# Eight attention batches and their expert layer on one core: the second softmax turned by way of DRAM instead of on TensorE, and batch 0's state read moved into batch 1

## The chip, the cores and the metric

The kernel runs on one core of a Trainium2 chip. The core has a matrix engine (TensorE, PE in the profile, with PEld for its weight loads), a vector engine (VectorE, DVE), a scalar engine (ScalarE, ACT), GpSimd (POOL) and SyncE (SP), which here only issues DMAs. The metric is the device time of one execution in microseconds (us); lower is better. The kernel before takes 654.04 us, the median of 3 runs (653.77 to 654.39).

## The reference, cut to what matters

An attention between 512 tokens and 32 state rows, both ways, for 8 batches of 8 heads of 64 numbers, and then one expert layer over all 4352 rows (512 tokens and 32 state rows of each batch), with 512 inputs, 2048 hidden numbers and 512 outputs:

```python
scores = scale * np.matmul(x, state.transpose(0, 1, 3, 2))     # x: 8, 8, 512, 64
a = softmax(scores)                                            # state: 8, 8, 32, 64
xread = np.matmul(a, state)
scores2 = scale * np.matmul(state, x.transpose(0, 1, 3, 2))
a2 = softmax(scores2)
sread = np.matmul(a2, x)
rows = np.concatenate([xread, sread], axis=2)                  # per head: 512 + 32 rows
...
h = rows @ w_in                                                # 512 -> 2048
g = np.where(h >= 1, h, np.where(h <= -1, 0.0, (h + 1) ** 2 / 4))
return g @ w_out                                               # 2048 -> 512
```

All of it is float32. scores2 is scores turned; both softmaxes work from the same numbers.

## The kernel before, in words

**Precision.** A float32 product is made of three passes with shorter factors: each operand is kept as a high part (h) and a rest (l), and high times high, high times rest and rest times high are summed in PSUM. So every product stands in the rows as three matmuls: L446 to L448 for the first layer (g1, output h), L504 to L506 for the second (g2, output acc).

**Attention folded into the weights.** xread @ w_in is a @ (state @ w_in). So for each batch the kernel forms sw = state @ w_in (`sw_pair`, L393), splits it (swh, swl), and g1 multiplies the first softmax (its high part ath and its rest atl, tokens on the columns) by sw. The first softmax goes on DVE and ACT: `turn` (L237) turns 32x32 blocks of the scores out of PSUM, then maximum, difference, exp, sum, division (top1 to norm1), `back` (L276) turns the result back, `high1` and `rest` split it. The hidden activation follows on ACT and DVE: relu (L455), square (L458), bound (L462), high part gh (L468), rest gl (L473).

**The second softmax**, the one that the change is about, runs over the tokens, which lie on the columns of the scores tile sc: `top2` (L294, L295) takes the maximum of a row on DVE, `exp2` (L298) writes exp and its sum on ACT into the tile e2, state rows on partitions. To read x with it, the tokens must lie on the partitions. `turn2` (L309) does that on TensorE: eight 128x128 transposes per batch into a PSUM tile e2p, which `keep_turned` (L313) copies back over e2 on ACT. Then `read2` (L327) multiplies it with xn, the batch's x with tokens on partitions, in 32 matmuls into sr; `scale2` (L335) divides by the sum; `keep2` (L341) turns the 128x128 result on TensorE; `keep` (L346) stores it in srT. After the last batch the 256 state rows collected in srT pass through the expert layer as a ninth batch of half the steps.

**Steps.** The 2048 hidden numbers are taken in 8 steps j of 256 each. A step has 12 matmuls 128x512 of g1 and 24 of g2; g2 of a step follows g1 of the next, in two parts with other PE work between them (sw of a later step, scores and read2 of a batch).

**Order of the work.** Batches 1 to 8 are written as a loop over steps (b, j), in which the framework's scheduler sets the order on each engine. Batch 0 has a hand-written order: `Plan` holds a list of operations, each with engine, cost, what it waits for and which buffers it takes; the table `ORDER` names them in the order of emission by their number and engine letter; `Plan.times` (from L63) works out a modelled start for each; `Plan.emit` issues them sorted by that start and puts dummy matmuls into warmed (`warm`, L175, "fills") where the model leaves PE idle between the first scores and the first g2. In this stretch the weights come in on SP's queue, 1 MB at a time: raw_i0 to raw_i7 (w_in) in two buffers of the pool rawp, raw_o0 to raw_o7 (w_out) in eight buffers of wop. Each is 64-bit data that two operations turn into float32 halves (`low` L545/L550 on DVE or ACT, `high` L558 on ACT) and that DVE joins (L566) into w32 (w_in) or into wf, a tile of the pool "tmp" (w_out), from which `part_high` (L573, ACT) and `part_low` (L577, DVE) make the two parts of wo, in a buffer of wop again. xt is x for the scores, sb the state, xn x for read2; each comes on SP's queue.

The dictionary `between` says with which step of batch 0 the attention's own PE work is listed: `turn2` of batch 0 with step 0, `read2` with step 1 (between the two halves of g2 of step 0), the scores of batch 1 with step 2, `keep2` with step 3, and `turn2` of batch 1 with step 4.

**PSUM.** Two tiles for h (one of two banks in batch 0), four for acc, and one tile mm of two banks that scores, sw, e2p, sr of batch 0 and rt take in turn.

Of the kernel before, what the change touches and what calls it, by code (L numbers as in the profile page):

```python
# [108 lines left out]
def state_exchange_moe(  # L109
# [91 lines left out]

    class Attention:
# [82 lines left out]

        def top2(self, q):
            b = self.b
            if q == 0:
                tag = "tmp" if b == 0 else "e2"
                self.e2 = work.tile([P, 2, S], F32, tag=tag, bufs=2 if b == 0 else 1, name=f"e2_{b}")  # L290
                self.nm2 = small.tile([P, 2], F32, tag="nm2", name=f"nm2_{b}")
                self.sum2 = small.tile([P, 2], F32, tag="sum2", name=f"sum2_{b}")
# [1 line left out]
            nc.vector.tensor_reduce(out=nm, in_=self.sc[q], op=ALU.max, axis=AX.X, negate=True)  # L294
            nc.vector.tensor_scalar_mul(nm, nm, SCALE)  # L295

        def exp2(self, q):
            nc.scalar.activation(  # L298
                out=self.e2[:, q], in_=self.sc[q], func=AF.Exp, bias=self.nm2[:, q:q + 1],
                scale=SCALE, accum_out=self.sum2[:, q:q + 1],  # L300
            )

        def turn2(self):
            b, e2 = self.b, self.e2
            e2p = self.e2p = ps_mm(f"e2p{b}")
            for q in range(2):
                for t in range(NT):
                    cols = slice(t * P, (t + 1) * P)
                    nc.tensor.transpose(out=e2p[:, q, cols], in_=e2[:, q, cols], identity=ident)  # L309

        def keep_turned(self):
            b = self.b
            nc.scalar.copy(out=self.e2, in_=self.e2p)  # L313
# [558 lines left out]
```

## Time and profile before

| what | value |
|---|---|
| median of 3 runs | 654.04 us (653.77 to 654.39) |
| the profiled execution's own time | 653.93 us |
| its span (first to last instruction) | 651.9 us |
| PE busy | 642.5 us, 99% of the span |
| PEld busy | 521.2 us, 80% |
| ACT busy | 362.3 us, 56% |
| DVE busy | 338.1 us, 52% |
| the chain that ended last | PE 96%, DVE 2%, ACT 1% |
| DMA | 43.64 MB, mean 67 GB/s |

The profile is one execution, taken by the hardware profiler. A row of the trace gives start and length in us, engine, line of the kernel, operation, out<-in by the program's names, and the shape; a release in brackets says how long the engine was idle before the instruction and what ended that. Matmuls overlap, so the lengths of neighbouring matmuls add up to more than the time between their starts. A row of groups gives busy time and mean length in ns, and behind the second bar the idle time just before the group's instructions. A row of stretches gives the window, its length, then for PE, PEld, DVE, ACT and POOL busy us and number of instructions, then the TensorE clock that was granted as a share of full speed, the DMA engines' share and GB/s.

### The profile page before, as it was taken

What the parts mean: (1) busy time and instruction counts of PE and PEld (TensorE: products, weight loads), DVE (VectorE), ACT (ScalarE), POOL (GpSimd) and SP (SyncE); (2) the same over time, 40 slices, a digit from 0 to 9 for tenths busy, and PEclk for the clock granted to TensorE, in tenths of its full rate; (3) what the DMA queues carried; (4) which work ended last, traced back from release to release, by engine and by line L of the source; (5) the groups of instructions that cost most, each with busy time, mean ns of one, the idle gap of its engine ahead of it and who ended that gap; (6) DMA issues with size and microseconds to landing.
All of it is one profiled execution on the core that took longest, in us unless ns stands there. A gap on an engine that the chain in (4) does not pass through costs nothing.

```text
span 651.9 us, 10329 instructions
## 1 busy us (share of the span) xinstructions
PE 642.5 (99%) x4438; PEld 521.2 (80%) x4438; DVE 338.1 (52%) x484; ACT 362.3 (56%) x474; POOL 0.8 (0%) x7
## 2 busy tenths in 40 slices
PE   7999999999999999999999999999999999999997
PEld 6777887878787887878787887878787878788895
DVE  5999958533584338443574339343663334334431
ACT  5999766554565456454664457444664464444632
POOL 0000000000000000000000000000000000000000
PEclk9999999999999999999999999999999999999999
DMA  8996005000400004000500014000300010000101
GB/s 347 387 401 253 1 10 185 0 1 2 168 27 1 1 32 163 0 2 2 193 2 1 1 46 149 1 2 1 130 1 1 0 67 1 0 2 1 64 1 33
DMA packets 11085, 43.64 MB, mean 67 GB/s; under 512 B 1312, under 2 KB 1440, under 8 KB 7968
## 3 DMA queue, kind: packets, MB, share of 16 engines
q1 hardware_dynamic: 6096, 34.28, 13.6%
q10 hardware_dynamic: 4944, 8.72, 3.6%
q8 instruction: 34, 0.56, 0.4%
q14 instruction: 11, 0.09, 0.0%
HBM read 34.08 MB, written 8.91 MB: 66 GB/s over the span
## 4 chain that ended last, share of the span: by engine, by line
PE 96%; DVE 2%; ACT 1%; DMA 0%; issue 0%; POOL 0%; SPq 0%; DVEq 0%; POOLq 0%
PE acc L504 19%; PE acc L505 19%; PE acc L506 19%; PE h L446 10%; PE h L447 10%; PE h L448 10%; PE sw L393 5%; PE sc L230 1%; PE warmed L175 1%; PE sr L327 1%; PE e2p L309 1%; DVE w L566 0%; DVE u L462 0%; DMA out_dram<-o 0%; DVE z L237 0%; DVE z L252 0%
## 5 line engine op out<-in xcount | busy, mean ns | idle before, releaser
L504 PE MATMUL acc<-wo,gh 128*128 128x512 f32 x544 | 214.0, 393 | 0.0
L505 PE MATMUL acc<-wo,gh 128*128 128x512 f32 x544 | 212.1, 390 | 0.0
L506 PE MATMUL acc<-wo,gl 128*128 128x512 f32 x544 | 211.9, 390 | 0.0
L455 ACT ACTIVATE u<-h,half 128x512 f32<-128x512 f32 (+1 forms) x128 | 91.7, 717 | 178.3 <-PE h L448 170.2
L462 DVE SCALAR_TENSOR_TENSOR u<-u,h 128x512 f32<-128x512 f32 (+1 forms) x128 | 86.4, 714 | 199.8 <-ACT u L458 199.6
L504 PEld LDWEIGHTS acc<-wo,gh 128*128 128x128 f32 x544 | 102.2, 188 | 24.4 <-issue 3.3
L506 PEld LDWEIGHTS acc<-wo,gl 128*128 128x128 f32 x544 | 102.1, 188 | 21.6
L505 PEld LDWEIGHTS acc<-wo,gh 128*128 128x128 f32 x544 | 102.2, 188 | 20.6 <-DVE wo L577 0.2
L473 DVE TENSOR_TENSOR gl<-u,gh 128x1024 fp32r<-128x1024 f32 x68 | 83.2, 1224 | 56.5 <-ACT gh L468 56.5
L468 ACT CAST gh<-u 128x1024 fp32r<-128x1024 f32 x68 | 71.5, 1052 | 66.0 <-DVE u L462 63.4
L458 ACT ACTIVATE u<-u 128x1024 f32<-128x1024 f32 x68 | 72.1, 1061 | 1.8
L393 PE MATMUL sw<-w,sb 64*32 64x256 f32 x1024 | 32.3, 380 | 2.5 <-DVE w L566 2.5
L393 PEld LDWEIGHTS sw<-w,sb 64*32 64x32 f32 x1024 | 18.2, 106 | 11.9 <-DVE u L462 2.5
L519 ACT COPY o<-acc 128x512 f32<-128x512 f32 x33 | 19.0, 583 | 12.1 <-PE acc L506 12.1
L446 PE MATMUL h<-ath,sw_3h 128*128 128x512 f32 x64 | 25.1, 393 | 0.0
L446 PE MATMUL h<-ath,sw_5h 128*128 128x512 f32 x64 | 25.0, 391 | 0.0
L447 PE MATMUL h<-ath,sw_5l 128*128 128x512 f32 x64 | 24.9, 389 | 0.0
L448 PE MATMUL h<-atl,sw_5h 128*128 128x512 f32 x64 | 24.9, 389 | 0.0
L447 PE MATMUL h<-ath,sw_3l 128*128 128x512 f32 x64 | 24.9, 389 | 0.0
L448 PE MATMUL h<-atl,sw_3h 128*128 128x512 f32 x64 | 24.9, 389 | 0.0
L446 PE MATMUL h<-ath,sw_1h 128*128 128x512 f32 x60 | 24.4, 407 | 0.5 <-DVE u L462 0.5
L447 PE MATMUL h<-ath,sw_1l 128*128 128x512 f32 x60 | 23.4, 391 | 0.0
(158 smaller groups left out, 722.5 us busy)
## 6 DMA issues: line engine op xcount, KB each, us to landing
xt<-in_xt_dram SPq DMA_DIRECT2D x16, 512.0 KB, 5.2
raw_i<-in_moe_w_in_dram SPq DMA_DIRECT2D x8, 1024.0 KB, 7.0
raw_o<-in_moe_w_out_dram SPq DMA_DIRECT2D x8, 1024.0 KB, 11.4
xn<-in_x_dram SPq DMA_DIRECT2D x8, 1024.0 KB, 6.1
out_dram<-o ACTq DMA_DIRECT2D x32, 256.0 KB, 2.0
sb<-in_state_dram SPq DMA_DIRECT2D x1, 448.0 KB, 8.5
out_dram<-o SPq DMA_DIRECT2D x4, 64.0 KB, 1.7
out_dram<-o ACTq DMA_DIRECT2D x4, 64.0 KB, 2.0
```

The costliest lines, as they stand in the source:

```text
L393: nc.tensor.matmul(banks[hh][pr * NS:(pr + 1) * NS, cols], lhsT=sb[rows, b, pr], rhs=w32[c][rows, pr], start=True, stop=True,)
L446: nc.tensor.matmul(o, lhsT=wh[:, k, sl], rhs=ah[:, k], start=first, stop=False)
L447: nc.tensor.matmul(o, lhsT=wl[:, k, sl], rhs=ah[:, k], start=False, stop=False)
L448: nc.tensor.matmul(o, lhsT=wh[:, k, sl], rhs=al[:, k], start=False, stop=last)
L455: nc.scalar.activation(out=u, in_=h, func=AF.Relu, scale=0.5, bias=half)
L458: nc.scalar.activation(out=self.u, in_=self.u, func=AF.Square)
L462: nc.vector.scalar_tensor_tensor(out=u, in0=u, scalar=1.0, in1=h, op0=ALU.min, op1=ALU.max)
L468: nc.scalar.copy(out=gh, in_=self.u)
L473: nc.vector.tensor_tensor(out=gl, in0=self.u, in1=gh.bitcast(F32), op=ALU.subtract)
L504: nc.tensor.matmul(a, lhsT=lh, rhs=oh, start=f == 0, stop=False)
L505: nc.tensor.matmul(a, lhsT=lh, rhs=ol, start=False, stop=False)
L506: nc.tensor.matmul(a, lhsT=ll, rhs=oh, start=False, stop=f == NF - 1)
```

## The change

Three things change together.

**The block trade, all batches.** `turn2` and `keep_turned` go. In their place `trade` issues DMAs on SP's queue: e2 is stored to a DRAM tile e2d (one store of 128x1024; two of 512 KB in all for batch 0), and four loads bring it back as e2x, a tile of the pool "tmp", so that each quarter of 128 tokens lies on its own 32 partitions with the pairs of heads side by side. `turn_traded` then turns 32x32 blocks of the whole 128x1024 tile in one DVE instruction, which gives tokens on partitions, written over e2. To match, x is laid out on the host with token 128 t + 32 j + k at partition 32 t + k, group j (the DMA of xn has the same size), and exp2 of batches 1 to 7 writes e2 with the two halves of the heads interleaved by quarters. The trade is issued right after exp2, the DVE turn stands where turn2 was called (`first`, step 2 of the batch before). The number of e2 buffers goes from one to two.

**Batch 0.** ACT copies its scores aside (`aside`) from PSUM to e2_0, so that PSUM is free; top2 and exp2 work there in place, later. read2, scale2, keep2 and keep of batch 0 leave the hand-written part and stand behind those of batch 1, in steps 0 and 1 of batch 1. They share the PSUM bank of sr1 and the tile of rt1. `between` keeps only the scores of batch 1. xn0 takes a buffer of rawp and is loaded behind all weights.

**The order.** A new table ORDER; `emit` issues the operations in the table's order, not sorted by their modelled start. The operation "table" (a copy of one column) stands last for ACT. The space for DMA descriptors is given as 8192.

The diff without most of the table, and without what only passes names on:

```diff
@@ ORDER @@
-    "0S 87P 86A 1S 2S 88P 6S 97D 90D 89P 91D 99D 92D 10S 93D 100D 94D 3A 98D 101D 95A 33S 102A 96D "
+    "0S 87P 88P 90D 1S 89P 113A 97D 91D 2S 98D 99D 92D 100D 116A 121A 93D 6S 101D 3A 102A 4D 94D 95A "
...
@@ Plan.emit @@
-        for k in sorted(begun, key=lambda k: begun[k]):
+        for k in begun:
...
@@ load_xn @@
-        xn = work.tile([P, NT, H, D], F32, tag="xn", bufs=1, name=f"xn{b}")
+        if b:
+            xn = work.tile([P, NT, H, D], F32, tag="xn", bufs=1, name=f"xn{b}")
+        else:
+            xn = rawp.tile([P, NT, H, D], F32, tag="raw", name=f"xn{b}")
...
@@ Attention @@
+        def aside(self, q):
+            if q == 0:
+                self.e2 = work.tile([P, 2, S], F32, tag="e2", name=f"e2_{self.b}")
+            nc.scalar.copy(out=self.e2[:, q], in_=self.sc[q])
...
         def exp2(self, q):
+            if self.b:
+                o, i = self.e2[:, :, q], self.sc[q].rearrange("p (t k) -> p t k", k=P)
+            else:
+                o = i = self.e2[:, q]
...
-        def turn2(self):
-            b, e2 = self.b, self.e2
-            e2p = self.e2p = ps_mm(f"e2p{b}")
-            for q in range(2):
-                for t in range(NT):
-                    cols = slice(t * P, (t + 1) * P)
-                    nc.tensor.transpose(out=e2p[:, q, cols], in_=e2[:, q, cols], identity=ident)
-
-        def keep_turned(self):
+        def trade(self):
+            self.e2x = work.tile([P, NPR, 2 * P], F32, tag="tmp", name=f"e2x{self.b}")
+            there = dram.tile([P, NT, 2 * P], F32, tag="e2d", name=f"e2d{self.b}")
+            if self.b:
+                nc.sync.dma_start(out=there, in_=self.e2.rearrange("p t q k -> p t (q k)"))
+            else:
+                for q in range(2):
+                    nc.sync.dma_start(
+                        out=there[:, :, q * P:(q + 1) * P], in_=self.e2[:, q].rearrange("p (t k) -> p t k", k=P)
+                    )
+            for t in range(NT):
+                nc.sync.dma_start(
+                    out=self.e2x[t * NS:(t + 1) * NS], in_=there[:, t].rearrange("(r n) k -> n r k", n=NS)
+                )
+
+        def turn_traded(self):
+            e2 = self.e2.rearrange("p t q k -> p (t q k)" if self.b else "p q s -> p (q s)")
+            nc.vector.transpose(out=e2, in_=self.e2x.rearrange("p r k -> p (r k)"))
+            self.turned = e2.rearrange("p (r q j n) -> p r q j n", q=2, r=NPR, n=NS)
+            self.inv2()
...
             for q in range(2):
                 self.exp2(q)
+            self.trade()
...
-            self.turn2()
-            self.keep_turned()
+            self.turn_traded()
...
@@ att_ops2 @@
+                op(("aside",) + k, "ACT", 0.66, m("aside", q), [("sc", b, 1)] + [("aside", b, 0)] * q, take=take, ends=[("sc", b)])
...
+        op(("trade", b), "SP", 6.5, m("trade"), [("exp2", b, 0), ("exp2", b, 1)], take=[("tmp", ("e2x", b))])
+        op(("kept", b), "DVE", 1.3, m("turn_traded"), [("trade", b)], ends=[("e2x", b)])
...
@@ the loads @@
-    read(("xn", 0), 2.6, load, "xn", load_xn, 0, take=[("xn", ("xn", 0))])
...
+    weights = [k for k in plan.ops if k[0] == "dma" and k[1] in ("i", "o")]
+    read(("xn", 0), 2.6, load, "xn", load_xn, 0, take=[("raw", ("xn", 0))], after=weights)
...
@@ between @@
-        0: lambda: tensor(("e2p", 0), 0.92, lambda: atts[0].turn2(), [("exp2", 0, 0), ("exp2", 0, 1)],
-                          take=[("mm", ("e2p", 0))]),
-        1: lambda: tensor(("sr", 0), 1.23, lambda: atts[0].read2(), [("kept", 0), ("dma", "xn", 0)],
-                          take=[("mm", ("sr", 0))], ends=[("e2", 0), ("xn", 0)]),
...
-        3: lambda: tensor(("rt", 0), 0.15, lambda: atts[0].keep2(), [("rs", 0)], take=[("mm", ("rt", 0))]),
-        4: lambda: tensor(("e2p", 1), 0.92, lambda: atts[1].turn2(), [("exp2", 1, 0), ("exp2", 1, 1)],
-                          take=[("mm", ("e2p", 1))]),
...
@@ the loop over steps (b, j), j = 0 and j = 1 @@
-                atts[b].read2()
-                atts[b].scale2()
+                for k in (1, 0) if b == 1 else (b,):
+                    atts[k].read2()
+                for k in (1, 0) if b == 1 else (b,):
+                    atts[k].scale2()
...
@@ _laid_out @@
-        "x": x.reshape(B, H, S // 128, 128, D).transpose(0, 3, 2, 1, 4),
+        "x": x.reshape(B, H, 4, S // 128, 32, D).transpose(0, 2, 4, 3, 1, 5).reshape(B, 128, S // 128, H, D),
```

Lines of the changed kernel lie some 33 further down: a g2 matmul of L504 to L506 is L537 to L539 there, g1 L479 to L481, scores L235, read2 L358.

What that moves on the engines is seen at three places. First PE in batch 0, from the end of h of step 1 to the first g2 products, before (acc0_0 is the first output tile of g2, wo0 the weights of step 0, gh0_0 and gl0_0 the parts of its activation, e2p0 the turned second softmax):

```order
L448 MATMUL h0_1_297<-atl0_118,sw0_1h_235 128x512
L309 MATMUL e2p0_319<-ident_76,e2_0_247 128x128 x8
L504 MATMUL acc0_0_334<-wo0_314,gh0_0_304 128x512
L505 MATMUL acc0_0_334<-wo0_314,gh0_0_304 128x512
L506 MATMUL acc0_0_334<-wo0_314,gl0_0_305 128x512
L504 MATMUL acc0_1_335<-wo0_314,gh0_0_304 128x512
```

and in the same place after:

```order
L481 MATMUL h0_1_298<-atl0_117,sw0_1h_252 128x512
L537 MATMUL acc0_0_321<-wo0_270,gh0_0_292 128x512
L538 MATMUL acc0_0_321<-wo0_270,gh0_0_292 128x512
L539 MATMUL acc0_0_321<-wo0_270,gl0_0_293 128x512
L537 MATMUL acc0_1_322<-wo0_270,gh0_0_292 128x512
```

The eight turns are gone, and g2 follows h of step 1 at once. Twelve rows further down, before, the read of batch 0 (sr0) stood between the two halves of g2(0, 0) and h of step 2 begins behind it; after, the second half of g2(0, 0) follows the first and then h of step 2.

Second, PE at the first h of batch 1 and at the read of batch 1, before (sc2 are the scores of batch 2, sr1 the read of batch 1):

```order
L505 MATMUL acc0_3_337<-wo6_744,gh0_6_789 128x512
L506 MATMUL acc0_3_337<-wo6_744,gl0_6_790 128x512
L446 MATMUL h1_0_0_888<-ath1_466,sw0_7h_678 128x512
...
L506 MATMUL acc0_3_337<-wo7_821,gl0_7_871 128x512
L327 MATMUL sr1_946<-xn1_579,e2_1_495 32x64 x32
L393 MATMUL sw1_1_0_981<-w32_1_91,sb_88 32x256
```

and after:

```order
L538 MATMUL acc0_3_324<-wo6_684,gh0_6_763 128x512
L539 MATMUL acc0_3_324<-wo6_684,gl0_6_764 128x512
L235 MATMUL sc2_1017<-xt2_846,sb_90 32x512
L479 MATMUL h1_0_0_850<-ath1_420,sw0_7h_639 128x512
...
L539 MATMUL acc0_3_324<-wo7_828,gl0_7_833 128x512
L358 MATMUL sr1_908<-xn1_737,e2_1_473 32x64 x32
L358 MATMUL sr1_908<-xn0_616,e2_0_142 32x64 x32
L426 MATMUL sw1_1_0_977<-w32_1_93,sb_90 32x256
...
L426 MATMUL sw1_3_1_998<-w32_4_96,sb_90 32x256
L235 MATMUL sc2_1017<-xt2_846,sb_90 32x512 x7
L479 MATMUL h1_1_0_1061<-ath1_420,sw1_1h_979 128x512
```

The read of batch 0 stands behind that of batch 1. One of the eight score matmuls of batch 2 has come to stand alone ahead of h of batch 1; the other seven stand where all eight stood.

Third, the end of the weights on SP's queue (what a DMA waits for before it is issued is in brackets, by semaphore), before:

```order
L538 DMA raw_i7_544<-in_moe_w_in_dram 128x2048 [waits DMAHW7_49,DMAHW5_49,DVE_49]
L538 DMA raw_o5_564<-in_moe_w_out_dram 128x2048 [waits DMAHW6_49]
L199 DMA xn1_579<-in_x_dram 128x2048 [waits PE_49]
L194 DMA xt2_884<-in_xt_dram 128x1024 [waits DMAHW0_49,PE_49]
L194 DMA xt2_884<-in_xt_dram 128x1024 [waits DMAHW1_49]
```

and after:

```order
L571 DMA raw_i7_544<-in_moe_w_in_dram 128x2048 [waits DMAHW0_49,DVE_49]
L196 DMA xt2_846<-in_xt_dram 128x1024 [waits DMAHW5_49,PE_49]
L196 DMA xt2_846<-in_xt_dram 128x1024 [waits DMAHW6_49]
L571 DMA raw_o5_613<-in_moe_w_out_dram 128x2048 [waits DMAHW7_49,DVE_49,Activation_49]
L204 DMA xn0_616<-in_x_dram 128x2048 [waits DMAHW2_49]
L323 DMA e2d1_708<-e2_1_473 128x1024 [waits DMAHW1_49]
L330 DMA e2x1_707<-e2d1_708 32x4x256 [waits DMAHW1_49,DVE_49]
L330 DMA e2x1_707<-e2d1_708 32x4x256 [waits DMAHW3_49]
L330 DMA e2x1_707<-e2d1_708 32x4x256 [waits DMAHW4_49]
```

xt2 moves ahead of the last weight, that weight now waits for another engine, and xn0 and the trades of batches 1 and 0 stand behind it.

More of the change, by code (lines that the diff above doesn't have):

```diff
@@ L288, in top2 @@
             if q == 0:
[L289 to L292, printed above, removed]
+                if b:
+                    self.e2 = work.tile([P, NT, 2, P], F32, tag="e2", name=f"e2_{b}")
+                first = "" if b else "_0"
+                self.nm2 = small.tile([P, 2], F32, tag=f"nm2{first}", name=f"nm2_{b}")
@@ L311, in keep_turned @@
-        def keep_turned(self):
+                out=o, in_=i, func=AF.Exp,
+                bias=self.nm2[:, q:q + 1], scale=SCALE, accum_out=self.sum2[:, q:q + 1],
+            )
+        def trade(self):
[12 more added lines that the diff above has]
+                )
@@ L312, in keep_turned, with inv2 @@
+        def turn_traded(self):
[3 more added lines that the diff above has]
+            self.inv2()
+        def inv2(self):
             b = self.b
-            nc.scalar.copy(out=self.e2, in_=self.e2p)
-            self.r2 = small.tile([P, 2], F32, tag="r2", name=f"r2_{b}")
+            self.r2 = small.tile([P, 2], F32, tag="r2" if b else "r2_0", name=f"r2_{b}")
@@ L320, in read2 @@
             xn = loaded.pop(("xn", b))
-            sr = banks[1].tile([P, 512], F32, tag="h", name=f"sr{b}") if b else ps_mm(f"sr{b}")[:, 0]
-            sr = self.sr = sr[:, :2 * D].rearrange("p (q d) -> p q d", q=2)
+            if b:
+                self.read = banks[1].tile([P, 512], F32, tag="h", name=f"sr{b}")
+            else:
+                self.read = atts[1].read
+            at = 0 if b else 2 * D
+            sr = self.sr = self.read[:, at:at + 2 * D].rearrange("p (q d) -> p q d", q=2)
             for q in range(2):
-                for t in range(NT):
+                for j in range(NT):
                     for pr in range(NPR):
-                        c0 = t * P + pr * NS
                         nc.tensor.matmul(
-                            sr[pr * NS:(pr + 1) * NS, q], lhsT=self.e2[:, q, c0:c0 + NS],
-                            rhs=xn[:, t, 2 * pr + q], start=t == 0, stop=t == NT - 1,
+                            sr[pr * NS:(pr + 1) * NS, q], lhsT=self.turned[:, pr, q, j],
+                            rhs=xn[:, j, 2 * pr + q], start=j == 0, stop=j == NT - 1,
                         )
@@ L339, in keep2 @@
         def keep2(self):
-            self.rt = ps_mm(f"rt{self.b}")
+            b = self.b
+            self.turned2 = ps_mm(f"rt{b}") if b else atts[1].turned2
+            self.rt = self.turned2[:, 0 if b else 1, :P]
             nc.tensor.transpose(
-                out=self.rt[:, 0, :P], in_=self.rs.rearrange("p a d -> p (a d)"), identity=ident
+                out=self.rt, in_=self.rs.rearrange("p a d -> p (a d)"), identity=ident
             )
@@ L648, in att_ops2 @@
             k = (b, q)
-            take = [("tmp" if b == 0 else "e2", ("e2", b))] if q == 0 else []
-            op(("top2",) + k, "DVE", 0.8, m("top2", q), [("sc", b) if b else ("sc", b, 1)] + [("top2", b, 0)] * q, take=take)
-            op(("exp2",) + k, "ACT", 0.66, m("exp2", q), [("top2",) + k], ends=[("sc", b)])
-        op(("kept", b), "ACT", 0.95, m("keep_turned"), [("e2p", b)], ends=[("e2p", b)])
-        if b == 0:
-            op(("rs", b), "DVE", 0.25, m("scale2"), [("sr", b)], ends=[("sr", b)])
-            op(("srT", b), "ACT", 0.3, m("keep"), [("rt", b)], ends=[("rt", b)])
+            take = [("e2", ("e2", b))] if q == 0 else []
+            if b:
+                ready, used = [("sc", b)], [("sc", b)]
+            else:
+                op(("aside",) + k, "ACT", 0.66, m("aside", q), [("sc", b, 1)] + [("aside", b, 0)] * q, take=take, ends=[("sc", b)])
+                take, ready, used = [], [("aside", b, q)], []
+            op(("top2",) + k, "DVE", 0.8, m("top2", q), ready + [("top2", b, 0)] * q, take=take)
+            op(("exp2",) + k, "ACT", 0.66, m("exp2", q), [("top2",) + k], ends=used)
+        op(("trade", b), "SP", 6.5, m("trade"), [("exp2", b, 0), ("exp2", b, 1)], take=[("tmp", ("e2x", b))])
+        op(("kept", b), "DVE", 1.3, m("turn_traded"), [("trade", b)], ends=[("e2x", b)])
     hid = {}
@@ L734, in state_exchange_moe @@
     att_ops2(0)
-    op(("sc done", 0), "ACT", 0, lambda: None, [("exp2", 0, 0), ("exp2", 0, 1)])
+    op(("sc done", 0), "ACT", 0, lambda: None, [("aside", 0, 0), ("aside", 0, 1)])
     sw_ops((0, 0))
@@ L812, in state_exchange_moe @@
         elif j == 1:
-            atts[b].keep2()
-            atts[b].keep()
+            for k in (1, 0) if b == 1 else (b,):
+                atts[k].keep2()
+            for k in (1, 0) if b == 1 else (b,):
+                atts[k].keep()
         elif j == 2 and nxt:
```

15 lines of the change are left out of this document (8 added, 7 removed), and 22 rows, old and new, of the table ORDER.

## The prediction

> **What bounds the kernel now.** I read the page first, then the busy time by stretches, then the instructions of TensorE (PE) one by one around each place that the change touches. Starts are us from the span's start.
>
> ```profile
> span 651.9 us, 10329 instructions
> PE 642.5 (99%) x4438; PEld 521.2 (80%) x4438; DVE 338.1 (52%) x484; ACT 362.3 (56%) x474; POOL 0.8 (0%) x7
> PE 96%; DVE 2%; ACT 1%; DMA 0%; issue 0%; POOL 0%; SPq 0%; DVEq 0%; POOLq 0%
> ...
> 40.00:50.00 10.00, 10.00 (x56) 7.37 (x55) 9.88 (x13) 9.96 (x10) 0.00 (x0) 1.00 0.98 387
> 100.00:172.50 72.50, 72.50 (x521) 58.41 (x513) 35.42 (x54) 38.59 (x54) 0.00 (x0) 1.00 0.12 44
> ```
>
> The chain that ended last is 96% PE. The stretches (behind the window: PE, PEld, DVE, ACT, POOL, clock, DMA share, GB/s) show two regimes. From 100 us on a batch takes 72.5 us, PE is busy in all of it, DVE and ACT in half: there a TensorE instruction less is worth its pitch, and work on other engines costs nothing. While the weights come in (40 to 50 us is shown) PE, DVE, ACT and DMA are all full: there PE gains from work taken off it only as far as the others deliver earlier too.
>
> **The turns that go.** A busy PE overstates matmuls, which overlap, so each block is costed by the pitch of its neighbours. First the pitch, then the block of batch 2, then that of batch 0 (start, length):
>
> ```profile
> 37.49 0.39 PE L504 MATMUL acc<-wo,gh 128*128 128x512 f32 x1
> ...
> 39.99 0.39 PE L506 MATMUL acc<-wo,gl 128*128 128x512 f32 x1
> ```
> ```profile
> 117.67 0.39 PE L506 MATMUL acc<-wo,gl 128*128 128x512 f32 x1
> 117.90 1.03 PE L309 MATMUL e2p<-ident,e 128*128 128x128 f32 x8
> 118.69 0.48 PE L504 MATMUL acc<-wo,gh 128*128 128x512 f32 x1
> ...
> 119.24 0.40 PE L506 MATMUL acc<-wo,gl 128*128 128x512 f32 x1
> ```
> ```profile
> 28.08 0.39 PE L448 MATMUL h<-atl,sw_1h 128*128 128x512 f32 x1
> 28.31 1.03 PE L309 MATMUL e2p<-ident,e 128*128 128x128 f32 x8
> 29.10 0.48 PE L504 MATMUL acc<-wo,gh 128*128 128x512 f32 x1
> ...
> 30.05 0.40 PE L504 MATMUL acc<-wo,gh 128*128 128x512 f32 x1
> ```
>
> Twelve matmuls, eleven steps in 2.50: 0.227 us a step. From 117.67 to 119.24 are 1.57 us with three ordinary steps (0.68) in them: a block of eight turns costs 0.89. **Batches 1 to 7: 7 x 0.89 = 6.23 us off.** Batch 0: 28.08 to 30.05 is 1.97, less four steps (0.91), so 1.06.
>
> The Trainium skill (TensorE: Matmul & The Clock Gate, Back-to-back issue gap) gives about 81 ns for a matmul of 128 columns in a stream of loads and matmuls; by it eight blocks of eight would be worth 5.2 us. The trace has 0.79 us from a block's start to the next matmul, 0.10 a turn, before the edges: the row decides.
>
> Batch 0's block also covered a wait, since the g2 behind it needs gl0_0 and wo0:
>
> ```profile
> 20.84 0.70 DVE L545 TENSOR_SCALAR raw_i<-raw_i 128x1024 int32<-128x1024 uint32 x1 [0.65 <-DMA raw_i<-in_moe_w_in_dram]
> 27.06 1.21 DVE L473 TENSOR_TENSOR gl<-u,gh 128x1024 fp32r<-128x1024 f32 x1
> 28.20 1.22 DVE L577 TENSOR_TENSOR wo<-wf,wo 128x1024 fp32r<-128x1024 f32 x1
> ```
> ```profile
> 21.96 1.10 ACT L455 ACTIVATE u<-h,half 128x1024 f32<-128x1024 f32 x1
> ```
> ```profile
> L298 ACT ACTIVATE e<-sc,nm 128x512 f32<-128x512 f32 x16 | 10.9, 684 | 1.7 <-DVE nm L295 1.7
> L313 ACT COPY e<-e2p 128x1024 f32<-128x1024 f32 x8 | 8.1, 1014 | 0.1
> L294 DVE TENSOR_REDUCE nm<-sc 128x1 f32<-128x512 f32 x16 | 10.2, 665 | 0.0
> ```
>
> raw_i2 lands at 20.84; behind it ACT makes its high part and the first relu (21.96). In the new order five 1-MB transfers still lie ahead of raw_i2 and its high part still stands ahead of that relu, so relu stays near 22. From there to gl, ACT loses the two exp2 of batch 0 (2 x 0.68) and gains a sw cast and the wo0 cast, which move in ahead of gh: about even, so gl is done where it was, 27.06 + 1.21 = 28.27. DVE makes wo0 ahead of gl now, in the 1.3 us that the two top2 (2 x 0.67) leave. So the first g2 starts at 28.3 instead of 29.10, and PE waits some 1 us ahead of it. I take **0.85 off** (0.75 to 1.06).
>
> The two copies aside stand at the head of ACT's row, ahead of raw_i0's high part, and one of DVE's turns stands behind the first of them. An exp2 of the same size takes 0.68; one of these can make the softmax late by that much, and DVE's 0.65 us of waiting for raw_i2 absorbs it: nothing, at most 0.7.
>
> **The read of batch 0 moves.** Before, alone between a g2 and an h; after, behind sr1 in batch 1. What it cost, and what sr1 costs from its start to the sw product:
>
> ```profile
> 31.90 0.40 PE L506 MATMUL acc<-wo,gl 128*128 128x512 f32 x1
> 32.23 1.10 PE L327 MATMUL sr<-xn,e 128*32 128x64 f32 x64
> 33.40 0.50 PE L446 MATMUL h<-ath,sw_2h 128*128 128x512 f32 x1
> ...
> 34.20 0.40 PE L446 MATMUL h<-ath,sw_2h 128*128 128x512 f32 x1
> ```
> ```profile
> 99.55 1.10 PE L327 MATMUL sr<-xn,e 128*32 128x64 f32 x64
> 100.58 1.96 PE L393 MATMUL sw<-w,sb 64*32 64x256 f32 x64
> ```
>
> 31.90 to 34.20 is 2.30, less four steps 1.39. Paid back at 99.55 to 100.58 without new edges: 1.03. **0.36 off.** The turn rt0 moves next to rt1 and changes nothing that I can price.
>
> **A score matmul stands alone.** In the built order one of the eight instructions of sc2 stands ahead of h1_0, seven where all eight stood. Scores run as row and column tiles side by side, two passes deep, so one alone holds PE nearly as long as eight. The nearest row is batch 1's whole block, which also stands between a g2 and an h:
>
> ```profile
> 40.30 1.09 PE L230 MATMUL sc<-xt,sb 64*32 64x512 f32 x16
> 41.33 0.50 PE L446 MATMUL h<-ath,sw_3h 128*128 128x512 f32 x1
> ...
> 42.12 0.40 PE L446 MATMUL h<-ath,sw_3h 128*128 128x512 f32 x1
> ```
>
> From the matmul at 39.99, quoted above, to 42.12 is 2.13, less four steps 1.22. Sixteen records there are eight matmuls of two passes; one matmul has both passes. The rest of the block still needs its two passes. **1.2 on** (0 if PE had to wait for h1_0's input there anyway; it can't gain).
>
> **The trade.** Per batch 512 KB go out and come back on SP's queue, and DVE transposes 128x1024 between gl of step 2 and u of step 3. Here is that place in batch 1, then two prices:
>
> ```profile
> 119.00 1.23 DVE L473 TENSOR_TENSOR gl<-u,gh 128x1024 fp32r<-128x1024 f32 x1
> 125.58 1.28 DVE L462 SCALAR_TENSOR_TENSOR u<-u,h 128x512 f32<-128x512 f32 x2 [5.36 <-ACT u L458]
> 128.04 1.23 DVE L473 TENSOR_TENSOR gl<-u,gh 128x1024 fp32r<-128x1024 f32 x1 [1.17 <-ACT gh L468]
> ```
> ```profile
> 108.60 0.20 ACT L298 ACTIVATION_READ_ACCUMULATOR e<-sc,nm 128x1 f32 x1
> 132.18 0.39 PE L506 MATMUL acc<-wo,gl 128*128 128x512 f32 x1
> ```
> ```profile
> L276 DVE STREAM_TRANSPOSE zt<-z 128x512 f32<-128x512 f32 x16 | 10.6, 694 | 0.1
> xn<-in_x_dram SPq DMA_DIRECT2D x8, 1024.0 KB, 6.1
> ```
>
> The transpose is 2 x 0.69 = 1.4 us in 5.36 idle: nothing. The round trip may last from exp2's end (108.8) to 120.2, 11.4 us, before DVE waits, 5.36 - 1.4 = 4 more before u is late, and 2.9 more (gl done 129.27, used at 132.18) before PE is. A store and loads of half a megabyte each cost at most two times the 6.1 of a megabyte: 12.2, nothing on PE. What SP holds behind the trade (xn, xt of the next batch) waits for PE's reads a batch later.
>
> In batch 0 the queue has a knot. raw_o5 takes the slot of raw_o4, which is free only when DVE has joined wf4; xn0 and batch 1's trade stand behind it. In the new row of DVE the join comes some 4 us ahead of raw_o5's first use, a megabyte takes up to 6.1 to land: DVE may wait 0 to 1.5 us, g2 of step 4 has nearly as much in hand. I add 0.1, and keep 1.5 for the range.
>
> **Sum.** 6.23 + 0.85 + 0.36 - 1.2 - 0.1 = 6.1 us off. The profiled execution took 653.93 (span 651.9, 2.0 around it), the median of three runs is 654.04: 654.0 - 6.1 = **647.9**. What a measurement can tell from no change is 0.2%, 1.3 us.
>
> **Rivals.**
>
> *The cheap single.* The lone sc2 matmul falls into a wait for h1_0, or one tile costs PE 0.2; batch 0's whole 1.06 is won: 654.0 - 6.23 - 1.06 - 0.36 + 0.2 = 646.6. For: an order made outside the hand-written row may put it where PE idles. Against: nothing in the trace of before waits at h1_0, and DVE has no more to do ahead of it now than a 1.4 us transpose.
>
> *The full stretch gives way.* ACT and DVE, 98% busy at 40 to 50 us, must serve PE 2.2 us earlier. They lose in that stretch ACT's eviction of e2p0 (1.01) and two exp2 (1.4), and DVE's two top2 (1.3), about that much; but one operation of 1.2 us on the wrong side, or raw_o5's 1.5, shows on PE. Or the clock falls:
>
> ```profile
> 13.00:14.00 1.00, 0.00 (x0) 0.00 (x0) 1.00 (x2) 1.00 (x2) 0.00 (x0) 1.00 1.02 418
> 15.00:16.00 1.00, 1.00 (x7) 1.00 (x6) 1.00 (x3) 1.00 (x3) 0.00 (x0) 0.50 0.72 197
> ```
>
> After two idle us the clock was 0.50 in 15 to 16. The new row has 14 fills before sw0_0 and 14 before h0_0, so idle spells of 1 to 2 us are left, and h0_0's twelve matmuls now stand in one piece; at half clock they take 12 x 0.227 = 2.7 longer, of which the wait for raw_i2 hides about 1. Price 1.2 to 2.7: 649 to 650.6, say 649.8. The Trainium skill (TensorE: Matmul & The Clock Gate, Why this matters for your kernels) asks for gaps above some 3 us before the clock falls; by it nothing is lost here. The rows show it falling after 2.0.
>
> *The late trade (slower).* If the round trip passes 11.4 + 4 + 2.9, about 18 us from exp2, PE waits in each of six batches: at 20 us that is 2 x 6 = 12 on, 660. For: the loads are issued only after the store has landed, on one queue. Against: 12.2 at the most by the row above.
>
> *No gain.* The turns are off PE, but another chain keeps the old pace (gl of step 1, say, with the least room): 654. Against: PE idle is zero in 100 to 172.5.
>
> **Chances.** Forecast 0.66 (its own range 646.9 to 648.9), cheap single 0.12, full stretch 0.14, late trade 0.04, no gain 0.04. The range 645.9 to 650.4 takes the first two and most of the third, about 0.9. Faster by over 0.2%: 0.92; within: 0.04; slower: 0.04.
>
> **What would show it.** Right: no L309 group, stretches of 71.6 us per batch, PE idle still zero from 100 us on, a 64-record sr block followed by a second one, a lone sc block of two records ahead of h1_0 that moves the next matmul by about 1.2, and a first g2 near 28.3. Wrong: DVE idle ahead of its 128x1024 transpose with the releaser a DMA, PE waiting for gl or wo between 30 and 90 us, or a clock of 0.50 under h0_0.

## The result and the profile after

The changed kernel takes 646.99 us, the median of 4 runs (646.61 to 647.40), against 653.98 for the kernel before (653.77 to 654.39): 7.0 us less, a ratio of 0.9892 with a 95% interval of 0.9875 to 0.9910. The forecast was 647.9, in a range of 645.9 to 650.4. The profiled execution took 647.03.

First the page of the changed kernel (its span, the busy times, the chain that ended last), then of its stretches one while the weights come in and one batch of the steady part.

```profile
span 645.3 us, 10268 instructions
PE 635.3 (98%) x4372; PEld 513.1 (80%) x4372; DVE 347.0 (54%) x492; ACT 355.2 (55%) x468; POOL 0.8 (0%) x7
PE 95%; DVE 2%; ACT 1%; issue 0%; DMA 0%; ACTq 0%; POOL 0%; SPq 0%; POOLq 0%
```
```profile
40.00:50.00 10.00, 10.00 (x56) 7.34 (x55) 9.47 (x12) 9.97 (x12) 0.00 (x0) 1.00 0.82 323
100.00:171.60 71.60, 71.60 (x510) 57.47 (x495) 36.67 (x57) 37.75 (x53) 0.00 (x0) 1.00 0.16 55
```

A batch takes 71.6 us where it took 72.5, and PE is still busy in all of it. In the batch shown DVE has 1.25 us more work (36.67 against 35.42, the 128x1024 transpose) and ACT 0.84 less (37.75 against 38.59, the copy of e2p): both engines have half the batch free, and neither shows in the time.

The three places of PE's row that the prediction costed, in the changed kernel (start, length): the end of h of step 1 with the first g2, the lone score matmul ahead of the first h of batch 1, and the two reads with what follows.

```profile
28.57 0.39 PE L481 MATMUL h<-atl,sw_1h 128*128 128x512 f32 x1
28.79 0.39 PE L537 MATMUL acc<-wo,gh 128*128 128x512 f32 x1
...
29.47 0.39 PE L537 MATMUL acc<-wo,gh 128*128 128x512 f32 x1
...
87.99 0.39 PE L539 MATMUL acc<-wo,gl 128*128 128x512 f32 x1
88.31 1.04 PE L235 MATMUL sc<-xt,sb 64*32 64x512 f32 x2
89.28 0.50 PE L479 MATMUL h<-ath,sw_7h 128*128 128x512 f32 x1
...
97.68 1.99 PE L358 MATMUL sr<-xn,e 128*32 128x64 f32 x128
99.61 1.96 PE L426 MATMUL sw<-w,sb 64*32 64x256 f32 x64
101.36 1.06 PE L235 MATMUL sc<-xt,sb 64*32 64x512 f32 x14
102.35 0.50 PE L479 MATMUL h<-ath,sw_1h 128*128 128x512 f32 x1
```

The first g2 follows h of step 1 at one pitch, at 28.79 (before: 29.10). Two records of scores hold PE 0.97 us up to the next h, and the fourteen that are left take 0.99: seven matmuls cost what eight did. The two reads together take 1.93 where one took 1.03.

And the trade of batch 2 in the changed kernel: its rows on SP's queue, its rows on DVE, and from the answer for the tile e2x how long its loads took to land.

```profile
108.55 0.33 SPq L323 DMA_DIRECT2D e2d<-e  x1
111.21 1.75 SPq L330 DMA_DIRECT2D e2x<-e2d  x4
```
```profile
119.27 1.24 DVE L336 STREAM_TRANSPOSE e<-e2x 128x1024 f32<-128x1024 f32 x1
123.82 1.28 DVE L495 SCALAR_TENSOR_TENSOR u<-u,h 128x512 f32<-128x512 f32 x2 [3.32 <-ACT u L491]
```
```profile
DMA to landing us min/median/max: 2.6/2.9/3.9
```

The store goes out as exp2 ends, the loads 2.7 us later, and the last of them, issued by 112.96, lands by about 115.9. DVE turns the tile at 119.27 with no idle time ahead of it: some 3.4 us are left over, and 3.3 of idle time stand behind.

**Where the time went.** Starts of PE's blocks give the account of the two profiled executions (653.93 and 647.03, 6.90 apart). Up to the first g2: 29.10 against 28.79, 0.31 off. From there to the first h of batch 1: 62.20 against 60.49, 1.71 off; 0.27 of this still lies at the first g2: the three steps behind it take 0.95 before (29.10 to 30.05, shown in the prediction), where a part of wo0 was done only at 29.42, and 0.68 after (28.79 to 29.47). From that h to the one of step 1 (91.30 to 103.33, 89.28 to 102.35): 12.03 against 13.07, 1.04 on. From there to the first h of batch 7 (526.30 and 520.00), with the six blocks of turns of batches 2 to 7 in it: 422.97 against 417.65, 5.32 off. To PE's last matmul 0.12 on; behind it and around the span (653.93 - 647.31 and 647.03 - 641.13) 6.62 against 5.90, 0.72 off, which no step of the change is known to touch. In the profiles of the experiments below this last part lies between 5.8 and 6.7 (6.6 and 6.7 in the two kernels with seven hops), so a difference of this size comes by chance.

### The profile page after: what moved, and what is told of

It reads as the page before. It is cut to its first block, busy times and chain, and to the rows that moved or that the text cites. A ratio compares the mean times of both kernels' runs of the same rounds, so it can differ in the third digit from the quotient of the medians.

```text
span 645.3 us, 10268 instructions
## 1 busy us (share of the span) xinstructions
PE 635.3 (98%) x4372; PEld 513.1 (80%) x4372; DVE 347.0 (54%) x492; ACT 355.2 (55%) x468; POOL 0.8 (0%) x7
## 4 chain that ended last, share of the span: by engine, by line
PE 95%; DVE 2%; ACT 1%; issue 0%; DMA 0%; ACTq 0%; POOL 0%; SPq 0%; POOLq 0%
PE acc L537 19%; PE acc L539 19%; PE acc L538 19%; PE h L479 10%; PE h L480 10%; PE h L481 10%; PE sw L426 4%; PE sc L235 1%; PE sr L358 1%; PE warmed L177 1%; DMA out_dram<-o 0%; ACT raw_o L591 0%; DVE z L274 0%; DVE sw_1l L442 0%; DVE m L253 0%
## 5 line engine op out<-in xcount | busy, mean ns | idle before, releaser
L537 PE MATMUL acc<-wo,gh 128*128 128x512 f32 x544 | 213.5, 392 | 0.0
L539 PE MATMUL acc<-wo,gl 128*128 128x512 f32 x544 | 211.8, 389 | 0.0
L537 PEld LDWEIGHTS acc<-wo,gh 128*128 128x128 f32 x544 | 102.1, 188 | 24.9 <-issue 3.7
L539 PEld LDWEIGHTS acc<-wo,gl 128*128 128x128 f32 x544 | 102.1, 188 | 21.6
L506 DVE TENSOR_TENSOR gl<-u,gh 128x1024 fp32r<-128x1024 f32 x68 | 83.3, 1224 | 55.3 <-ACT gh L501 55.3
L479 PE MATMUL h<-ath,sw_3h 128*128 128x512 f32 x64 | 25.1, 393 | 0.0
L479 PE MATMUL h<-ath,sw_5h 128*128 128x512 f32 x64 | 24.9, 390 | 0.0
L481 PE MATMUL h<-atl,sw_3h 128*128 128x512 f32 x64 | 24.9, 389 | 0.0
L481 PE MATMUL h<-atl,sw_5h 128*128 128x512 f32 x64 | 24.9, 389 | 0.0
L479 PE MATMUL h<-ath,sw_1h 128*128 128x512 f32 x60 | 24.4, 407 | 0.5 <-DVE u L495 0.4
L479 PE MATMUL h<-ath,sw_7h 128*128 128x512 f32 x60 | 23.5, 391 | 0.0
```

The source lines that it names most:

```text
L479: nc.tensor.matmul(o, lhsT=wh[:, k, sl], rhs=ah[:, k], start=first, stop=False)
L481: nc.tensor.matmul(o, lhsT=wh[:, k, sl], rhs=al[:, k], start=False, stop=last)
L506: nc.vector.tensor_tensor(out=gl, in0=self.u, in1=gh.bitcast(F32), op=ALU.subtract)
L537: nc.tensor.matmul(a, lhsT=lh, rhs=oh, start=f == 0, stop=False)
L539: nc.tensor.matmul(a, lhsT=ll, rhs=oh, start=False, stop=f == NF - 1)
```

## The experiments

Each kernel was timed beside the kernel before, which took 654.09 to 654.23 us there. Unless it is said otherwise the edit is made to the changed kernel.

### What a block of turns is worth: turns_back and trade_only

In the first, batches 2 to 7 are turned on PE again; x of these batches has the layout of before.

```diff
             for q in range(2):
                 self.exp2(q)
-            self.trade()
...
                 self.norm1(q)
-            self.turn_traded()
+            self.turn2()
+            self.keep_turned()
```

> The changed kernel with batches 2 to 7 turned on PE again as before (batches 0 and 1 traded). Theory: a block of eight turns costs PE 0.89 us and nothing covers it: 6 x 0.89 = 5.3 on, 652.3 us, and 72.5 us per batch again. Rival: the gain is mostly that of batch 0's moves and a turn is worth less than the trace says (81 ns each, 0.65 a block): 6 x 0.65 = 3.9 on, 650.9.

The second is the kernel before with the trade in these six batches alone; batches 0 and 1 stay as they were.

```diff
             for q in range(2):
                 self.exp2(q)
+            self.trade()
...
-            self.turn2()
-            self.keep_turned()
+            self.turn_traded()
```

> The kernel before with the trade in batches 2 to 7 alone, batches 0 and 1 as before. Theory: 6 x 0.89 = 5.3 off, 648.7 us, and 71.6 us per batch. Rival (a turn worth 81 ns): 3.9 off, 650.1. If both this and the turns put back agree with the theory, what the two batches 0 and 1 give is the rest of the change's 7.0: 1.7.

Measured: 652.17 us for turns_back (651.72 to 652.83; ratio to before 0.9966, 0.9954 to 0.9978) and 648.23 for trade_only (648.18 to 648.30; 0.9907, 0.9890 to 0.9923). One batch of each, turns_back first:

```profile
100.00:172.47 72.47, 72.47 (x510) 58.32 (x503) 35.45 (x56) 38.77 (x54) 0.00 (x0) 1.00 0.11 40
```
```profile
102.00:173.60 71.60, 71.60 (x508) 57.60 (x500) 36.57 (x55) 37.57 (x52) 0.00 (x0) 1.00 0.16 59
```

Six blocks put back cost 5.2 (652.17 - 646.99), six taken out of the kernel before bring 6.0 (654.19 - 648.23); the profiles, from the first h of batch 1 to that of batch 7, have 5.33 on and 5.44 off. So a block is worth about 0.89 and nothing covers it. The rival's 81 ns a turn are the figure of the Trainium skill (TensorE: Matmul & The Clock Gate, Back-to-back issue gap) quoted in the prediction. The trace does not agree: 5.32 us for 48 turns are 111 ns, and the measurement decides. What turns_back still keeps, the moves of batches 0 and 1, is worth 2.0 in the medians, but in PE's rows only 0.88 (its last matmul is done at 646.43, before at 647.31). The medians of both runs thus show more than the rows (6.0 against 5.44, 2.0 against 0.88), and I can't show why; starts that differ from execution to execution, told in the last section, are about large enough.

### The lone score matmul: sc_whole

```diff
-                nxt.scores()
+                if i == 0:
+                    behind = [k for k in nc.cur_bb.bb.instructions if k.engine == mybir.EngineType.PE][-1]
+                    with tc.issue_after(behind):
+                        nxt.scores()
+                else:
+                    nxt.scores()
```

> The changed kernel with all eight score matmuls of batch 2 in one piece behind sw1 in step 0 of batch 1, none ahead of h1_0; nothing else moves on PE. Theory: the lone one costs PE its whole place, 0.97 us from its start to h1_0 and 0.15 in the h block behind it, and the seven others still take the 0.99 of eight: 1.1 off, 645.9 us. Rival: PE would have to wait for h1_0's input at that place anyway: 647.0.

Measured: 646.37 us (645.75 to 647.50; 0.9880, 0.9865 to 0.9895). The two places in its profile:

```profile
88.38 0.39 PE L539 MATMUL acc<-wo,gl 128*128 128x512 f32 x1
88.60 0.39 PE L479 MATMUL h<-ath,sw_7h 128*128 128x512 f32 x1
...
100.53 1.10 PE L235 MATMUL sc<-xt,sb 64*32 64x512 f32 x16
101.56 0.50 PE L479 MATMUL h<-ath,sw_1h 128*128 128x512 f32 x1
```

From the first g2 (29.17 here) to the h of step 1 of batch 1 are 72.39 us, against 73.56 in the changed kernel: 1.17 off, as the theory has it. h1_0 follows g2 at one pitch, so there was no wait for the lone matmul to hide in. The medians show 0.6 of it, and the two intervals overlap: this kernel has the lowest median of all, and is clearly faster than the kernel before, but that it beats the changed kernel is shown by the place in the profile, not by the times. The runs' spread of 1.7 us is about as large as the step; the last section has a part of why.

### What stands ahead of the first g2: eight_before_g2, table_first, no_fills

```diff
-        tensor(("g2", half) + k, 2.74, lambda: g2(b, j, (4 * half, 4 * half + 4)), ...
+        def run():
+            if (b, j, half) == (0, 0, 0):
+                warm(8)
+            g2(b, j, (4 * half, 4 * half + 4))
+
+        tensor(("g2", half) + k, 2.74, run, ...
```

> The changed kernel with eight dummy matmuls of 128 columns ahead of the first g2, in the place of the turns of batch 0 that went. Theory after the trace: PE comes there straight from h of step 1 and waits for nothing, so they cost all of their 8 x 0.11 = 0.9 us: 647.9 us, first g2 at about 29.7. Rival, as the prediction had it: PE waits there about 1 us for the rest gl of step 0 and they hide in that: 647.0 to 647.3.

Measured: 649.15 us (648.62 to 649.52; 0.9920, 0.9905 to 0.9935).

```profile
28.60 0.40 PE L481 MATMUL h<-atl,sw_1h 128*128 128x512 f32 x1
28.83 1.95 PE L177 MATMUL warmed<-ident 128*128 128x128 f32 x16
30.54 0.48 PE L537 MATMUL acc<-wo,gh 128*128 128x512 f32 x1
```

The size in the expectation was wrong: a dummy matmul stands as two records, so eight are sixteen of 0.107 us, 1.71. But the question is answered: all of it reaches the first g2 (28.79 to 30.54), and none hides. PE has no wait there.

```diff
-    "0S 87P 88P 90D ...
+    "0S 87P 86A 88P 90D ...
-    ... 120D 86A "
+    ... 120D "
```

> The changed kernel with the operation table (a copy of one column, whose first use makes ACT load its function table for 1.28 us) at the head of ACT's row as before, not last. Theory: DVE's row is full from 8.1 us to the first g2, and an ACT that is free 1.3 us earlier is not what it waits for: 647.0 us, the first g2 within 0.3 of 28.8. Rival: ACT's late start (high part of raw_i0 at 10.11, before 8.27) is what makes h of steps 0 and 1 late: up to 1.3 off, 645.7.

Measured: 646.76 us (646.44 to 647.15; 0.9888, 0.9874 to 0.9903), the first g2 at 28.92. An ACT that loads its table while it is idle brings nothing that shows: the theory stands.

```diff
-                    if n > 0:
+                    if n > 0 and False:
                         fill(n)
```

> The changed kernel without the dummy matmuls between the first scores and the first g2 (the ten at the start stay). Theory (the clock falls in idle spells, as in the trace of before at 15 us): PE idles 7.9 to 13.5 and 14.1 to 17.9, the clock is 0.50 under h of step 0, twelve matmuls take 2.7 longer and more if it stays low: 649 to 652 us. Rival: DVE sets the pace up to the first g2 and a slower PE hides behind it, or the clock doesn't fall: 647.0.

Measured: 650.58 us (650.25 to 651.59; 0.9949, 0.9934 to 0.9964). Idle times, the first g2 and the clock (the last column but two of a stretch):

```profile
13.01 1.11 PE L426 MATMUL sw<-w,sb 64*32 64x256 f32 x16 [5.51 <-DVE w L599]
17.40 0.80 PE L479 MATMUL h<-ath,sw_0h 128*128 128x512 f32 x1 [3.28 <-ACT ath L284]
...
25.14 0.83 PE L426 MATMUL sw<-w,sb 64*32 64x256 f32 x16 [1.81 <-DVE sw_1l L442]
...
31.48 0.63 PE L481 MATMUL h<-atl,sw_1h 128*128 128x512 f32 x1
31.91 0.59 PE L537 MATMUL acc<-wo,gh 128*128 128x512 f32 x1
```
```profile
21.00:22.00 1.00, 1.00 (x4) 0.81 (x3) 1.00 (x2) 0.74 (x1) 0.00 (x0) 0.50 1.19 205
25.00:26.00 1.00, 0.83 (x16) 0.18 (x16) 0.73 (x2) 1.00 (x2) 0.00 (x0) 0.76 1.11 455
31.00:32.00 1.00, 1.00 (x4) 0.75 (x3) 0.81 (x1) 0.00 (x0) 0.00 (x0) 0.50 1.01 426
```

The clock falls to 0.50 within the 5.5 idle us (at 11.9) and is still there behind the next 3.3; it comes back at 22.1 and falls again at 25.5, after no more than 1.8 idle us. At 0.50 h steps at 0.43 instead of 0.23; the first g2 is 3.1 late, which is the 3.6 on the time but for the spread. In the changed kernel, with the fills, PE's longest idle spell in that stretch is 2.2, and the clock stays at 1.00 in its profile; in other profiles with these fills it did not, as the last section shows.

### How late a trade may be: three_hops, seven_hops, seven_held, sixteen_hops

Copies of e2d from DRAM to DRAM are put between store and loads of batches 2 to 7, one behind the other:

```diff
+            for i in range(3 if self.b > 1 else 0):
+                again = dram.tile([P, NT, 2 * P], F32, tag=f"e2d_{i}", bufs=1, name=f"e2d{self.b}_{i}")
+                nc.sync.dma_start(out=again, in_=there)
+                there = again
             for t in range(NT):
```

> The changed kernel with three more copies of e2d from DRAM to DRAM, one behind the other, between store and loads of batches 2 to 7. A trade takes 6.1 us from its store to its last landing and has 11.4 before DVE waits, 4 more before u of step 3 is late, 2.9 more before PE is. With three hops of some 2.7 us it takes 14.2. Theory: DVE waits about 3, PE nothing: 647.0 us. Rival (no slack behind DVE's wait): 6 x 3 = 18 on, 665.

> The changed kernel with seven more copies of e2d from DRAM to DRAM between store and loads of batches 2 to 7: a trade of 6.1 + 7 x 2.7 = 25 us. Theory (slack of 18 us from exp2): PE waits about 7 us in each of six batches, 42 on, 689 us, with DVE idle ahead of its 128x1024 transpose and a DMA as releaser. Rival (the trade is hidden however long, since PE's reads of it come a batch's length later): 647.

Measured: 647.31 us with three (647.25 to 647.48; 0.9897, 0.9881 to 0.9914) and 647.90 with seven (647.73 to 647.95; 0.9905, 0.9890 to 0.9920). The second answer is far from the 689 of the theory. With seven hops the loads are issued at 139.1 to 141.1, some 31 us after exp2, and DVE does wait:

```profile
139.24 0.68 DVE L287 TENSOR_TENSOR atl<-zt,ath 128x512 fp32r<-128x512 f32 x1
143.77 1.25 DVE L340 STREAM_TRANSPOSE e<-e2x 128x1024 f32<-128x1024 f32 x1 [3.85 <-DMA e2x<-e2d]
```

But it waits in another place: the scheduler has moved the transpose from behind gl of step 2 to behind gl of step 4, where PE waits for nothing. (With three hops it stands behind gl of step 3, at 127.97, and DVE does not wait for it at all, so that kernel does not test the slack either.) So the theory's slack, reckoned for a fixed row of DVE, was wrong for this program. Two more kernels separate the place from the lateness. seven_held is the kernel with seven hops with the transpose held where the changed kernel has it:

```diff
-            nc.vector.transpose(out=e2, in_=self.e2x.rearrange("p r k -> p (r k)"))
+            self.turn_at = nc.vector.transpose(out=e2, in_=self.e2x.rearrange("p r k -> p (r k)"))
...
-        g1(b, j)
+        if j == 3 and b + 1 < B:
+            with tc.issue_after(atts[b + 1].turn_at.ins):
+                g1(b, j)
+        else:
+            g1(b, j)
```

> The kernel with seven hops, but with the hidden step 3 of batches 1 to 6 issued on DVE behind the 128x1024 transpose, as it stands in the changed kernel's row. With seven hops alone the scheduler had moved that transpose behind step 4, where it waited up to 4.0 us a batch and cost PE almost nothing. Theory: it is the place in DVE's row that makes a late trade dear; the loads land at about 143.5 us, DVE holds u of step 3 until then, h of step 4 finds no bank at 127.3 and waits until 145.4: 18 in each of six batches, 109 on, some 756 us. The prediction's slack of 18 us from exp2 says 35 - 18 = 17 a batch, 750. Rival (a late trade is hidden wherever it stands): 648.

Measured: 762.67 us (760.87 to 763.44; 1.1653, 1.1635 to 1.1670).

```profile
144.81 1.24 DVE L340 STREAM_TRANSPOSE e<-e2x 128x1024 f32<-128x1024 f32 x1 [19.50 <-DMA e2x<-e2d]
...
146.68 0.80 PE L483 MATMUL h<-ath,sw_3h 128*128 128x512 f32 x1 [18.57 <-DVE u L499]
```
```profile
PE h L483 <- DVE u L499: 101.4, 7, 18.6
```
```profile
146.00:152.00 6.00, 5.32 (x13) 4.16 (x14) 2.45 (x4) 1.74 (x2) 0.00 (x0) 0.50 0.00 0
```

The same transfers, 115 us more. For some 101 of them, up to 18.6 in a batch, h finds no free bank, because u stands behind the waiting transpose; the rest fits the clock, which is 0.50 when PE goes on (the stretch from 146 to 152). sixteen_hops is the edit above with 16 for 3, and DVE's row free again:

> The changed kernel with sixteen more copies between store and loads of batches 2 to 7, DVE's row left to the scheduler, which puts the transpose ahead of gl of the next batch's step 0. A hop took 4.15 us with seven, so the loads land at 108.3 + 2.6 + 16 x 4.15 + 4.6 = 182, and the read of the batch stands at 171. Theory: the slack ends at that read, and with DVE's row free PE waits 182 + 1.2 - 171 = 12 in each of six batches, 72 on, 719 us. Rival (still hidden, or SP's queue moves later batches too): 648, or over 760.

Measured: 720.54 us (717.63 to 721.27; 1.0998, 1.0973 to 1.1024). The waits of its PE, the longest two:

```profile
PE sr L362 <- DVE e L340: 54.2, 6, 10.6
PE sw L430 <- DVE w L603: 2.2, 1, 2.2
```

Now PE waits for the transpose at the read of the next batch, in each of six batches, 54 us of the 74 that this kernel takes longer than the changed one; here too the clock is 0.50 when PE goes on. With DVE's row free a trade may take from exp2 (108) to that read (171), some 60 us; the changed kernel's takes 7.

### An earlier start: whole_warm8 and whole_warm5

Both are sc_whole with fewer dummy matmuls at the very start.

```diff
-WARM = 10
+WARM = 8
```

> The changed kernel with batch 2's scores in one piece and eight warm-up matmuls at the start, not ten. Theory: xt0's first half has landed at about 5.2 us, and the first scores stand at 6.01 only because 20 warm-up records of 0.213 us come ahead; with 16 the scores begin at about 5.2, DVE's first turns and the first g2 0.5 to 0.8 earlier (28.2): 645.9 - 0.6 = 645.4 us. Rival (the softmax waits for the second half of xt0 or for raw_i0, or the clock comes up later for it): 645.9 to 646.4.

> The same with five warm-up matmuls: PE is idle from about 3.6 to the landing of xt0. Theory: the first scores at 5.2 as with eight, no further gain: 645.4 us. Rival: the clock comes up later after the idle spell and the work up to the first g2 is slower, over 645.9.

Measured: 647.36 us with eight (646.87 to 647.85; 0.9894, 0.9880 to 0.9909) and 647.73 with five (647.70 to 647.99; 0.9901, 0.9886 to 0.9916). Of the kernel with eight, the first scores, the first g2, and PE's row behind the read of batch 1:

```profile
5.16 0.92 PE L235 MATMUL sc<-xt,sb 64*32 64x256 f32 x16
...
28.18 0.39 PE L537 MATMUL acc<-wo,gh 128*128 128x512 f32 x1
...
97.75 1.07 PE L426 MATMUL sw<-w,sb 64*32 64x256 f32 x24
99.87 1.28 PE L426 MATMUL sw<-w,sb 64*32 64x256 f32 x36 [1.05 <-issue]
```

Neither reaches the 645.4 of the theory. The start went as it has it: scores at 5.16, the first g2 at 28.18, 0.99 before that of sc_whole (not all of that need be the dummies': seven_hops, with ten of them, had its first g2 at 28.34). But 1.6 us were lost again between the first two h of batch 1 (14.58 against 12.96), in a stop of PE of 1.05 in the middle of sw for which the profile has no releaser. The kernel with five has the same stop, 1.1 long; its clock came up late besides (28 dummy records at 8.19 take 4.49 us, where they take 3.39 at full pace), and its first g2 is at 29.05. What stops PE there is open: the two kernels differ from sc_whole in the number of dummies alone, and no run was made on it.

## Why the prediction was right, step by step

- **Batches 1 to 7, 6.23 off: right.** Six of the seven blocks are 5.32 in the profile (5.34 forecast), and two kernels that move only them show 5.2 and 6.0.
- **The turns of batch 0, 0.85 off: 0.58 in the two profiles, and PE does not wait there.** From 30.05 to 29.47, the fourth product of g2 in both, are 0.58. The step that failed is "PE waits some 1 us ahead of it". gl of step 0 did end where the sum had it (27.02 + 1.23 = 28.25 in the changed kernel), but PE came later: h of step 1 began at 25.93, not 25.46, since it waits for the bank that bound of step 0 frees, and ended as g2 began. By the prediction's own rows, too, h of step 1 ends at 28.31 if it starts as before, just as g2 may start; the wait of 1 us stood on no row. eight_before_g2 shows that nothing is left to hide in. The forecast's 28.3 was not a wrong bound, though: the kernel with seven hops, the same up to batch 2, had its first g2 at 28.34. How large the gain is, two single executions can't tell, since this place moves from one to the next. Kernel trade_only has the rows of before up to here:

```profile
28.84 1.03 PE L315 MATMUL e2p<-ident,e 128*128 128x128 f32 x8
29.63 0.48 PE L528 MATMUL acc<-wo,gh 128*128 128x512 f32 x1
...
30.51 0.39 PE L528 MATMUL acc<-wo,gh 128*128 128x512 f32 x1
```

Against this the changed kernel is 1.04 ahead (30.51 to 29.47). So 0.85 is neither refuted nor confirmed, and no run moves the parts of batch 0 one by one.

- **The read of batch 0, 0.36 off: right in kind.** The second read costs 0.90 (1.93 - 1.03), not 1.03, so it is 0.49 off. The turn rt0, which I could not price, brings next to nothing: before, h of one step with rt0 in it took 2.96 us up to the sw behind it (61.76 to 64.72), after, the same without rt0 2.81 (62.47 to 65.28), which is 0.15; but the two turns together now cost 0.11 more than the one did. No run moves the read alone; this is read from the rows.
- **The lone score matmul, 1.2 on: right.** 0.97 and 0.15 in the h behind it; taken back by sc_whole, 1.17.
- **raw_o5, 0.1 on: nothing.** DVE waited 0.28 us for it, up to 63.12, inside the 0 to 1.5 allowed for; PE waits for no weight between 30 and 90 us.
- **The trade, nothing: right,** with 7 us where the bound had 12.2.
- **The sum, 6.1 off, against 6.9 and 7.0.** The steps inside PE's row make 6.18 of the profiles' 6.90. The 0.72 that are left lie behind the last matmul and around the span, and are within what single executions differ there. That the total came out 0.9 better than the forecast is therefore not shown to be the work of any step; part of it may be the start of the profiled execution of before, whose first g2 stood 0.53 earlier than the same one in trade_only.

**The rivals.** The cheap single (646.6) is nearest in time, but its mechanism is refuted: the single cost its whole 1.1. The full stretch did not give way in the changed kernel's profile: PE waits for nothing behind 28.8 us, and the clock stayed at 1.00. no_fills shows that the clock was a real danger, 3.6 us, and two other profiles with the same fills that it was not averted for good (last section). My reading, that 2.0 idle us bring the clock down, was too simple, however: the changed kernel idles 2.2 and keeps it. The rule that the prediction set against the row, gaps above some 3 us, is that of the Trainium skill (TensorE: Matmul & The Clock Gate, Why this matters for your kernels). The traces don't bear it out either: the clock fell after 1.8 idle us in no_fills, 2.0 in before and within the 2.2 of sc_whole, and the measurements decide. The late trade did not come, and its price was reckoned on a false ground: 18 us of slack hold only as long as DVE's row is kept.

## What to carry to other kernels

Where one engine is busy all the time, the worth of an instruction is the shift of its neighbours' starts, and it holds to a few hundredths; what is off that engine is free as long as its place in its own row is. A late transfer is dear by the instruction that waits for it and by what is queued behind that one: the same 31 us of lateness cost 0.9 us or 116 against the changed kernel. Small matmuls that run as tiles side by side are better kept together: here one alone cost 0.97 us, and eight 1.03.

## What the runs showed of the hardware

**TensorE's pace at the start changes from run to run.** The first dummies step at 0.213 us, later ones at 0.111. The clock's column says 1.00 in both, but the trace's first record of the clock begins only where the pace doubles. The same twenty records in the changed kernel, and in the one with seven hops:

```profile
1.45 4.64 PE L177 MATMUL warmed<-ident 128*128 128x128 f32 x20 [1.45 <-POOL ident masks.py:199]
```
```profile
1.45 4.20 PE L177 MATMUL warmed<-ident 128*128 128x128 f32 x20 [1.45 <-POOL ident masks.py:199]
```

The pace doubled at 4.5 us in the profile of before (twenty records in 3.92), at 5.0 with seven hops, and at 6.1, behind all twenty, in that of the changed kernel; the first scores stood at 5.30, 5.58 and 6.01, and of the two kernels with the same rows here, the one with seven hops had its first g2 0.45 earlier. So some 0.5 us of any comparison of two single executions of these kernels is luck. The Trainium skill (TensorE: Matmul & The Clock Gate, What's actually happening) says that the window after which the clock rises runs freely, so that the number of slow matmuls changes from run to run; the rows agree.

**A short idle spell may bring the clock down or not.** sc_whole and sixteen_hops have the changed kernel's row and its fills in this stretch. PE idles 2.2 us in all three, up to 13.4 to 13.9. Stretches of sc_whole and of sixteen_hops, and the first g2 of the latter:

```profile
15.00:16.00 1.00, 1.00 (x6) 1.00 (x6) 0.90 (x4) 1.00 (x3) 0.00 (x0) 0.50 0.67 172
```
```profile
27.00:28.00 1.00, 1.00 (x4) 0.81 (x3) 0.99 (x2) 1.00 (x2) 0.00 (x0) 0.50 1.10 459
```
```profile
30.51 0.39 PE L541 MATMUL acc<-wo,gh 128*128 128x512 f32 x1
```

In sc_whole the clock was 0.50 from 13.8 to 17.2; h of step 0 came 1.3 us later than in the changed kernel (19.14 against 17.88), the first g2 only 0.4. In sixteen_hops it was 0.50 from 26.4 to 29.8, after 1.3 idle us ahead of 24.7, and the first g2 came 1.7 later. In the changed kernel it did not fall. So the length of the idle spell alone does not decide it, and the price depends on what PE does then.

**Copies within DRAM.** Half a megabyte from DRAM to DRAM took about 4.1 us a hop (with seven hops the first is issued at 110.69, the loads behind the last at 139.09, each behind the landing of the one ahead), against 2.7 from store to loads.
